# The first pair's masks for both heads by one comparison of 128 partitions, its transfers in another order, its shift rows in two banks, and the last output block bank by bank

## The chip, the cores and the metric

The kernel runs on one core of a Trainium2 chip. The metric is the time of one execution on the device in microseconds (us), as the median of several runs. The profile is of one further execution; its span, from the first to the last instruction, is a little shorter than that execution's time.

The engines are PE (matrix multiply; PEld is its weight load), DVE (vector), ACT (scalar, activations), POOL (general) and SP (issues transfers). SP and ACT both issue DMA transfers here, each in the order of its own queue; SPq and ACTq are these issues in the profile.

## The reference

Attention in hash buckets, and then a feed-forward layer with a rational function:

```python
q_bits = (np.einsum('bhsd,dk->bhsk', q, proj) > 0)      # 6 bits a token; the same for k
mask = q_bucket[:, :, :, None] == k_bucket[:, :, None, :]
scores = np.where(mask, scale * np.matmul(q, k.transpose(0, 1, 3, 2)), -1000000000.0)
attn = np.exp(scores - np.max(scores, axis=-1, keepdims=True))
attn = attn / (np.sum(attn, axis=-1, keepdims=True) + 1e-09)
x = np.matmul(attn, v)                                  # 4 x 8 heads, 768 tokens, 64 each
# x as (3072, 512), then:
h = x @ w_in                                            # 512 -> 2048
g = (a[0] + a[1]*h + a[2]*h**2 + a[3]*h**3) / (1.0 + np.abs(b[0])*np.abs(h) + np.abs(b[1])*h**2 + 1e-6)
out = g @ w_out                                         # 2048 -> 512
```

## The kernel before

Everything is float32; a matmul that must be exact is made from a rounded high part and a low part (qh, ql, kh, kl, gh, gl). The 32 heads are worked in 16 pairs: the two heads of a pair lie on partitions 0 to 63 and 64 to 127. For each pair, `maxstep` makes 12 tiles of scores (psm) on PE, whose row maxima DVE takes (TENSOR_REDUCE, m<-psm); these give each query's shift. `scores` makes them again (pss) in transposed form, ACT takes the exponential (E<-pss), and `values` multiplies with v (psv). The bucket mask is a further matmul of 13 mask rows (mask_q, mask_k) that is added to the same sums, and one more row of mask_q carries the shift, against a row of ones in mask_k.

The mask rows come from the bits: PE multiplies Q and K with the projection (psb; for the first pair psb_first), and DVE compares with zero and subtracts a constant per partition (`TENSOR_SCALAR`, tile mb). For later pairs they are then moved to their partitions by four small transfers on SP (`maskrows`). The first pair uses no such transfers: `first_bits`, `first_compare`, `first_penalties` and `first_k_rows` make its rows in place, in two halves of 384 tokens (HQ), with engines copying head 0's rows to head 1's partitions; `first_shift` turns the maxima into the shift row on PE (pst) and copies it to rows 32 and 96 of mask_q. Until the first data is there, and in gaps, PE runs `warm(n)`: n matmuls on zeros (psw).

The order of all instructions is set by hand: the tables ZERO, ONE and so on hold a place for each step of each pair, `at` files steps by these numbers, and a loop issues them sorted; every engine then keeps program order. PSUM tiles of `ps_b` (tag s) share four banks.

After the last pair comes the feed-forward layer in 6 blocks of 512 tokens. `gemm2` adds the products of 16 parts f into four banks (pso, one for 128 tokens), each part by three matmuls a bank: gh with two weights, gl with one. POOL makes gl from gh. The last block's banks are copied out with a change of sign and stored (`store`).

The transfers at the start, word for word:

```python
queue.dma_start(QF[p][:, halves[0]], qT[p][:, halves[0]])
for c in halves:
    for h in range(2):
        q = nc.scalar if p == 0 and c.start == 0 and h == 1 else queue
        q.dma_start(KF[p][r, c], kT[p][64 - 64 * h : 128 - 64 * h, c])
```

Of the kernel before, what the change touches and what calls it, by code (L numbers as in the profile page):

```python
# [7 lines left out]
F32 = mybir.dt.float32  # L8
F32R = mybir.dt.float32r
# [3 lines left out]
AF = mybir.ActivationFunctionType  # L13
# [37 lines left out]
    penalties=[-94.565, -142.018], compare=-148.248, second=[[-145.217, -148.248], [-149.622, -154.85, -149.024, -148.687]],  # L51
# [99 lines left out]
def bucket_attention_then_rational_ffn(ctx, tc, qT, kT, v, proj, w_in, w_out, coef, consts, out):  # L151
# [70 lines left out]
    last = attention(tc, nc, raw, ps_b, tail, tokens, early, operands_to_terms, ffn, load, QF, KF, v, w_in, w_out, wo_d, ident, cst,  # L222
# [5 lines left out]
def attention(ctx, tc, nc, raw, ps_b, tail, tokens, early, operands_to_terms, ffn, load, QF, KF, v, w_in, w_out, wo_d, ident, cst, ones, prj,  # L228
# [31 lines left out]
    hs = sm.tile([32, 2], F32, name="hs")  # L260
    nc.vector.memset(hs[:, 0:1], 0.0)
    nc.vector.memset(hs[:, 1:2], BIG)
    nc.vector.memset(hs[0:14, 0:1], BIG)
    nc.vector.memset(hs[0:14, 1:2], 0.0)
# [95 lines left out]
    def first_bits(t, hf):  # L360
        if 0 not in MB:
            mb = sm.tile([P, 2, HQ], F32R, tag="mb", name="mb0")
            MB[0], MB[1] = (mb, 0), (mb, 64)
# [12 lines left out]
    def first_penalties(h, hf):  # L376
        rows, bits = MQ[0][64 * h : 64 * h + 32, hf * HQ : hf * HQ + HQ], MB[0][0][0:32, hf, :].bitcast(F32)
        if h == 1 and hf == 0:
            nc.gpsimd.tensor_scalar(out=rows, in0=bits, scalar1=hs[:, h : h + 1], scalar2=None, op0=ALU.mult)
        else:  # L380
            nc.scalar.activation(rows, bits, AF.Identity, scale=hs[:, h : h + 1])

    def first_k_rows(hf):
        c = slice(hf * HQ, hf * HQ + HQ)
        nc.scalar.copy(MK[0][64:96, c], MK[0][0:32, c].bitcast(F32))

    def first_shift(hf):
        c = slice(hf * HQ, hf * HQ + HQ)
        ps = ps_b.tile([P, 512], F32, tag="s", bufs=4, name=f"pst0_{hf}")
        for h in range(2):  # L390
            r = 64 * h + 32
            for i in range(NT // 2):
                j = NT * hf + 3 * h + i
                nc.tensor.matmul(ps[r : r + 1, i * P : i * P + P], M[0][:, j : j + 1], ident, start=True, stop=True)
        for h in range(2):
            r = 64 * h + 32
            if h:
                nc.scalar.activation(MQ[0][r : r + 1, c], ps[r : r + 1, 0:HQ], AF.Copy, scale=-1.0)
            else:
                nc.vector.tensor_scalar(out=MQ[0][r : r + 1, c], in0=ps[r : r + 1, 0:HQ], scalar1=-1.0, scalar2=None, op0=ALU.mult)  # L400
# [12 lines left out]
    def second_compare(hf):  # L413
        nc.vector.tensor_scalar(out=MB[1][0][64:128, hf, :], in0=AV.pop((1, hf))[64:128, 0:HQ], scalar1=0.0,
                                scalar2=cst[64:128, 0:1], op0=ALU.is_gt, op1=ALU.subtract)
# [124 lines left out]
    def at(p, s, f, *args):  # L540
        plan.setdefault(12 * p + s, []).append((f, args))
# [44 lines left out]
    warm(12)  # L586
    for h in range(2):
        nc.gpsimd.memset(MK[0][64 * h + 32 : 64 * h + 33].bitcast(F32), 1.0)
# [4 lines left out]
    for h in range(2):  # L593
        first_penalties(h, 0)
    first_k_rows(0)
# [5 lines left out]
    at(0, ZERO["second"][1][3], first_k_rows, 1)  # L601
# [5 lines left out]
    for hf in range(2):  # L607
        at(0, ZERO["combine"][hf], combine, 0, hf)
        at(0, ZERO["shift"][hf], first_shift, hf)
        at(0, ZERO["penalties"][hf], first_penalties, hf, 1)  # L610
# [4 lines left out]
    at(0, ZERO["compare"], first_compare, 0, 1)  # L615
    at(0, ZERO["clear"], first_clear)
# [77 lines left out]
class Ffn:  # L694
# [49 lines left out]
    def gemm2(self, t, f):  # L744
# [5 lines left out]
        if t == NBLK - 1 and f >= NFC - 2:  # L750
            order.sort(key=lambda ik: ik[1] == 2)
        for i, k in order:
# [5 lines left out]
            if f == NFC - 1 and k == 2:  # L758
                if end and i == n - 1:
                    self.store(t, i, 0, DM // 2, "scalar", nc.scalar)  # L760
                    self.store(t, i, DM // 2, DM, "vector", nc.sync)
                else:
                    self.store(t, i, 0, DM, "vector" if end and i % 2 else "scalar", nc.sync)

    def store(self, t, i, c0, c1, engine, queue):
        nc = self.nc
        if c1 - c0 < DM:
            o = self.tp.tile([P, DM], F32, tag="h2", name=f"oh{c0}_{t}_{i}", bufs=2)[:, 0 : c1 - c0]
        else:
            tag, bufs = ("sr", 1) if i % 3 == 2 else ("xo", 2)  # L770
            o = self.rows.tile([P, DM], F32, tag=tag, name=f"o{t}_{i}", bufs=bufs)[:, 0 : c1 - c0]
        ps = self.sums[t, i][:, c0:c1]
# [5 lines left out]
        queue.dma_start(self.out[r0 : r0 + P, c0:c1], o)  # L778
# [85 lines left out]
```

## Time and profile before

| | |
|---|---|
| median of 3 runs | 920.34 us (920.22 to 920.88) |
| the profiled execution | 919.83 us, its span 917.7 us |
| PE busy | 909.5 us, 99% of the span |
| DVE, ACT, POOL busy | 828.9, 654.4, 364.6 us (90%, 71%, 40%) |
| instructions | 15836 |

The page gives busy time by engine; PE is at work nearly all the time. Every instruction has the line of one helper (L140), so groups are told apart by tile names. In the timeline a row gives start, duration, engine, operation, output<-inputs with their shapes, and a count when several are merged; in brackets stand the idle time of the engine ahead of it and what ended it.

### The profile page before, as it was taken

The numbers are of one execution on the slowest core, as the hardware profiler recorded it, in microseconds if no ns is written. First come the engines' busy times: TensorE is split into PE (matmuls) and PEld (weight loads), VectorE is DVE, ScalarE is ACT, GpSimd is POOL, SyncE is SP. The second block draws the span as 40 slices with busy tenths as digits, with TensorE's granted clock in tenths as the row PEclk, the third lists the DMA queues.
The fourth block names the chain that finished last, engine by engine and source line by source line (L and its number), as shares of the span: only waits on it lengthen the run. The fifth ranks groups of instructions, "written<-read, shape, count | busy, mean of one in ns | idle before, by whom it ended". The sixth has DMA issues, their size and how long they took to land.

```text
span 917.7 us, 15836 instructions
## 1 busy us (share of the span) xinstructions
PE 909.5 (99%) x5838; PEld 725.5 (79%) x5838; DVE 828.9 (90%) x1062; ACT 654.4 (71%) x1228; POOL 364.6 (40%) x349
## 2 busy tenths in 40 slices
PE   9999999999999999999999999999999999999997
PEld 5678777787777787678888888888888888888886
DVE  7788889888988889898999999999999989998996
ACT  5577777777777777786777766776677676777664
POOL 6765655555555555412222232222222222222222
PEclk9999999999999999999999999999999999999999
DMA  6334444444444435355204000400040012001001
GB/s 170 89 125 146 147 144 148 145 149 142 151 141 152 142 118 173 120 197 194 103 1 132 7 0 1 139 1 1 7 131 1 1 62 77 1 1 46 1 0 46
DMA packets 39548, 81.50 MB, mean 89 GB/s; under 512 B 7216, under 2 KB 18596, under 8 KB 39472
## 3 DMA queue, kind: packets, MB, share of 16 engines
q1 hardware_dynamic: 38960, 80.18, 27.1%
q8 instruction: 46, 0.75, 0.3%
q10 hardware_dynamic: 512, 0.33, 0.1%
q14 instruction: 30, 0.25, 0.1%
HBM read 56.82 MB, written 21.17 MB: 85 GB/s over the span
## 4 chain that ended last, share of the span: by engine, by line
PE 95%; DMA 2%; DVE 2%; SPq 1%; ACT 1%; issue 0%; ACTq 0%
PE psh L140 29%; PE pso L140 28%; PE pss L140 13%; PE psv L140 13%; PE psm L140 7%; PE psu L140 2%; PE psb L140 1%; SPq L140 1%; DMA wo_d<-wr 1%; DMA mask_k<-mb 1%; PE psw L140 1%; DMA wr<-w_in 0%; ACT E L140 0%; DVE m L140 0%; DVE ws L140 0%
## 5 line engine op out<-in xcount | busy, mean ns | idle before, releaser
L140 POOL TENSOR_TENSOR gl<-c,gh 128x512 fp32r<-128x512 f32 x96 | 135.8, 1415 | 386.7 <-ACT gh L140 381.2
L140 PE MATMUL pso<-wo,gh 128*128 128x512 f32 x768 | 235.4, 389 | 0.0
L140 DVE TENSOR_REDUCE m<-psm 128x2 f32<-128x768 f32 x192 | 182.5, 958 | 19.6 <-PE psm L140 5.7
L140 ACT ACTIVATE E<-pss 128x384 f32<-128x384 f32 x384 | 167.1, 495 | 34.4 <-PE pss L140 27.7
L140 POOL TENSOR_TENSOR acc<-E,E 128x384 f32<-128x384 f32 x124 | 124.1, 1022 | 148.4 <-ACT E L140 147.6
L140 PEld LDWEIGHTS pso<-wo,gh 128*128 128x128 f32 x768 | 144.1, 188 | 29.8
L140 ACT ACTIVATE h<-psh 128x512 f32<-128x512 f32 x96 | 57.4, 598 | 130.9 <-PE psh L140 130.8
L140 PE MATMUL psh<-xh,wi_hi 128*128 128x512 f32 x384 | 149.6, 390 | 0.0
L140 PE MATMUL psh<-xl,wi_hi 128*128 128x512 f32 x384 | 149.4, 389 | 0.0
L140 PE MATMUL psh<-xh,wi_lo 128*128 128x512 f32 x384 | 149.4, 389 | 0.0
L140 PE MATMUL pso<-wo,gl 128*128 128x512 f32 x384 | 148.4, 389 | 0.0
L140 DVE SCALAR_TENSOR_TENSOR c<-c,ab,r 128x512 f32<-128x512 f32 x96 | 136.6, 1423 | 0.0
L140 PE MATMUL psv<-E,v 128*64 128x385 f32 x768 | 131.3, 490 | 0.0
L140 PEld LDWEIGHTS psv<-E,v 128*64 128x64 f32 x768 | 73.3, 137 | 45.9 <-issue 32.2
L140 POOL TENSOR_TENSOR acc<-acc,E 128x384 f32<-128x384 f32 x96 | 90.0, 958 | 4.0 <-ACT E L140 3.7
L140 DVE SCALAR_TENSOR_TENSOR w<-h,absb,w 128x512 f32<-128x512 f32 x96 | 75.0, 781 | 14.1 <-ACT w L140 13.7
L140 PEld LDWEIGHTS psh<-xh,wi_hi 128*128 128x128 f32 x384 | 72.1, 188 | 16.2 <-DVE c L140 0.6
L140 PEld LDWEIGHTS pso<-wo,gl 128*128 128x128 f32 x384 | 72.2, 188 | 15.0
L140 PEld LDWEIGHTS psh<-xl,wi_hi 128*128 128x128 f32 x384 | 72.1, 188 | 14.8
L140 PEld LDWEIGHTS psh<-xh,wi_lo 128*128 128x128 f32 x384 | 72.0, 188 | 15.0
L140 DVE SCALAR_TENSOR_TENSOR w<-w,r 128x512 f32<-128x512 f32 x96 | 78.5, 818 | 0.0
L140 ACT ACTIVATE c<-psh,ab 128x512 f32<-128x512 f32 x96 | 75.0, 781 | 0.7 <-POOL gl L140 0.7
(93 smaller groups left out, 1539.8 us busy)
## 6 DMA issues: line engine op xcount, KB each, us to landing
wr<-w_out SPq DMA_DIRECT2D x16, 512.0 KB
wr<-w_in SPq DMA_DIRECT2D x16, 512.0 KB
wo_d<-wr SPq DMA_DIRECT2D x16, 512.0 KB
wo<-wo_d SPq DMA_DIRECT2D x16, 512.0 KB
v<-v SPq DMA_DIRECT2D x16, 384.0 KB
x_d<-xo SPq DMA_DIRECT2D x32, 192.0 KB
out<-o SPq DMA_DIRECT2D x23, 256.0 KB
qkf<-qT SPq DMA_DIRECT2D x15, 384.0 KB
```

What stands on the lines that cost most here:

```text
L140: return self.tc.keep_in_program_order(issue(*args, **kwargs))
```

## The change

Four things change, all in the first 25 us or in the last 8.

1. *Masks of the first pair.* `first_bits` makes the bits of both heads: one bank for each of Q, K and each half, a matmul on zeros over all 128 partitions, and then one matmul with the projection for each head, into partitions 0 to 31 and 64 to 95. One comparison of 128 partitions with a new constant tile `first` gives all rows of both heads, the row of ones among them; one ACT instruction with `hs` gives the penalties of both heads. The copies of K's rows on ACT, the head-1 penalty on POOL, the memsets of the ones rows and the memset of the first mask tiles go. The second pair's mb is a tile of its own (mb1), which takes the place of the first's when that has been read. Of the 12 warm-ups ahead of the first bits 6 stay, and each of the two bits brings one matmul on zeros.
2. *Transfers.* Q's first half is issued by ACT, all of K by SP, prj after them; `first` comes by two small transfers on ACT, and cst by SP ahead of the second pair's Q and K.
3. *Shift rows.* `first_shift` writes the two heads' rows into two banks, and DVE copies head 0's, ACT head 1's.
4. *The last step.* In the last f of the last block, gl's matmuls of banks 0 and 1 follow directly on their gh ones, and banks 2 and 3 are then finished one by one. The last bank is copied whole by ACT and stored from ACT's queue, instead of in halves by ACT and DVE.

```diff
-        queue.dma_start(QF[p][:, halves[0]], qT[p][:, halves[0]])
+        (nc.scalar if p == 0 else queue).dma_start(QF[p][:, halves[0]], qT[p][:, halves[0]])
         for c in halves:
             for h in range(2):
                 r = slice(64 * h, 64 * h + 64)
-                q = nc.scalar if p == 0 and c.start == 0 and h == 1 else queue
-                q.dma_start(KF[p][r, c], kT[p][64 - 64 * h : 128 - 64 * h, c])
+                queue.dma_start(KF[p][r, c], kT[p][64 - 64 * h : 128 - 64 * h, c])
...
+    load(0)
     prj = cpool.tile([P, 2, 32], F32, name="prj")
     nc.scalar.dma_start(prj, proj)
-    load(0)
+    first = cpool.tile([P, 2], F32, name="first")
+    for h in range(2):
+        r = 64 * h + 32
+        nc.scalar.dma_start(first[r - 32 : r], consts[r - 32 : r + 32, 0:1].rearrange("(t r) o -> r (t o)", t=2))
+        nc.vector.memset(first[r : r + 32], 0.0)
+        nc.vector.memset(first[r : r + 1, 1:2], -1.0)
     cst = cpool.tile([P, 2 + P], F32, name="cst")
-    nc.scalar.dma_start(cst, consts)
+    nc.sync.dma_start(cst, consts)
...
-    for i in range(3):
+    for i in range(1, 3):
         for m in MASKS:
-            (nc.vector if i == 0 else nc.gpsimd).memset(m[i].bitcast(F32), 0.0)
+            nc.gpsimd.memset(m[i].bitcast(F32), 0.0)
...
     def first_bits(t, hf):
-        if (0, t) not in MS:
-            MS[0, t] = ps_b.tile([P, 512], F32, tag="s", bufs=4, name=f"psb_first{t}")
-        o = 64 * hf + 32 * t
-        nc.tensor.matmul(MS[0, t][o : o + 32, 0:HQ], prj[:, 0, :], (QF, KF)[t][0][:, hf * HQ : hf * HQ + HQ], start=True, stop=True)
+        ps = MS[0, t, hf] = ps_b.tile([P, 512], F32, tag="s", bufs=4, name=f"psb_first{t}_{hf}")
+        nc.tensor.matmul(ps[:, 0:HQ], spare[:, 0:P], spare[:, P:512], start=True, stop=True)
+        for h in range(2):
+            nc.tensor.matmul(ps[64 * h : 64 * h + 32, 0:HQ], prj[:, 0, :], (QF, KF)[t][0][:, hf * HQ : hf * HQ + HQ],
+                             start=True, stop=True)
 
     def first_compare(t, hf):
-        o = 64 * hf + 32 * t
...
-        out = MK[0][0:32, c] if t else MB[0][0][0:32, hf, :]
-        nc.vector.tensor_scalar(out=out, in0=MS[0, t][o : o + 32, 0:HQ], scalar1=0.0, scalar2=cst[o : o + 32, 0:1],
+        out = MK[0][:, c] if t else MB[0][:, hf, :]
+        nc.vector.tensor_scalar(out=out, in0=MS.pop((0, t, hf))[:, 0:HQ], scalar1=0.0, scalar2=first[:, t : t + 1],
                                 op0=ALU.is_gt, op1=ALU.subtract)
 
-    def first_penalties(h, hf):
...
+    def first_penalties(hf):
+        nc.scalar.activation(MQ[0][:, hf * HQ : hf * HQ + HQ], MB[0][:, hf, :].bitcast(F32), AF.Identity, scale=hs)
...
     def first_shift(hf):
-        ps = ps_b.tile([P, 512], F32, tag="s", bufs=4, name=f"pst0_{hf}")
+        ps = [ps_b.tile([P, 512], F32, tag="s", bufs=4, name=f"pst0_{hf}_{h}") for h in range(2)]
...
+        nc.vector.tensor_scalar(out=MQ[0][32:33, c], in0=ps[0][32:33, 0:HQ], scalar1=-1.0, scalar2=None, op0=ALU.mult)
+        nc.scalar.activation(MQ[0][96:97, c], ps[1][96:97, 0:HQ], AF.Copy, scale=-1.0)
...
-    warm(12)
-    for h in range(2):
-        nc.gpsimd.memset(MK[0][64 * h + 32 : 64 * h + 33].bitcast(F32), 1.0)
+    warm(6)
...
-            order.sort(key=lambda ik: ik[1] == 2)
+            order.sort(key=lambda ik: (ik[0] > 1 and f == NFC - 1) * (ik[0] + 1) + (ik[1] == 2))
...
-                if end and i == n - 1:
-                    self.store(t, i, 0, DM // 2, "scalar", nc.scalar)
-                    self.store(t, i, DM // 2, DM, "vector", nc.sync)
-                else:
-                    self.store(t, i, 0, DM, "vector" if end and i % 2 else "scalar", nc.sync)
+                last = end and i == n - 1
+                self.store(t, i, "vector" if end and i == 1 else "scalar", nc.scalar if last else nc.sync, last)
```

The table ZERO changes only where steps are gone or joined (penalties has one place, -142.018, and K's copy none).

Three places show what this does to the order on the engines. In the rows, a name ends with the number of its tile; DMAHW0 to DMAHW7 are eight counters that transfers use in turn, so a wait for one is a wait for the landing of an earlier transfer. First ACT's queue at the start, before:

```order
L140 ACT_TABLE_LOAD
L140 DMA prj_70<-proj 128x64
L140 DMA qkf0_72<-kT 64x384
L140 DMA cst_79<-consts 128x130
L140 CAST qh_0_213<-qkf0_72 128x384 [waits DMAHW0_49]
L140 CAST kh_0_219<-qkf0_72 128x384 [waits DMAHW5_49,DMAHW1_49]
L140 ACTIVATE mask_q0_164<-mb0_215,hs_189 32x384 [waits DVE_49]
```

and after:

```order
L140 ACT_TABLE_LOAD
L140 DMA qkf0_70<-qT 128x384
L140 DMA prj_77<-proj 128x64
L140 DMA first_79<-consts 32x2x1
L140 DMA first_79<-consts 32x2x1 [waits DMAHW0_49]
L140 CAST qh_0_210<-qkf0_70 128x384 [waits DMAHW3_49]
L140 CAST kh_0_218<-qkf0_70 128x384 [waits DMAHW1_49]
L140 ACTIVATE mask_q0_171<-mb0_216,hs_194 128x384 [waits DVE_49]
```

K's first half uses counters 0 and 1: the second transfer of `first` waits for the landing of one of its two pieces, and the casts stand behind it.

Second, ACT's queue around the first shift row (pst0), the scaling of the second pair's mb behind it, and the first exponentials (E), before:

```order
L140 ACTIVATE ws1_257<-wr1_256 128x512 [waits DMAHW3_49]
L140 ACTIVATE mask_q0_164<-mb0_215,hs_189 32x384
L140 ACTIVATE mask_q0_164<-pst0_0_319 1x384 [waits DVE_49]
L140 ACTIVATE mb0_215<-mb0_215,cst_79 64x768 [waits DMAHW7_49]
L140 ACTIVATE E3_155<-pss0_3_0_351 128x384 [waits PE_49]
```

and after:

```order
L140 ACTIVATE mask_q0_171<-mb0_216,hs_194 128x384 [waits DVE_49]
L140 ACTIVATE ws1_257<-wr1_256 128x512 [waits DMAHW5_49]
L140 ACTIVATE mask_q0_171<-pst0_0_1_324 1x384 [waits PE_49,Activation_49]
L140 ACTIVATE mb1_293<-mb1_293,cst_86 64x768 [waits DMAHW1_49,DVE_49,Activation_49]
L140 ACTIVATE E3_162<-pss0_3_0_356 128x384 [waits PE_49]
```

The shift row's wait for DVE has become one for PE, and the wait for DVE stands at mb.

Third, PE's last part (wo15; pso5_0 to pso5_3 are the four banks), before:

```order
L140 MATMUL pso5_0_9665<-wo15_5800,gh5_15_10187 128x512 [waits Activation_49]
L140 MATMUL pso5_0_9665<-wo15_5800,gh5_15_10187 128x512
L140 MATMUL pso5_1_9669<-wo15_5800,gh5_15_10187 128x512 x2
L140 MATMUL pso5_2_9673<-wo15_5800,gh5_15_10187 128x512 x2
L140 MATMUL pso5_3_9677<-wo15_5800,gh5_15_10187 128x512 x2
L140 MATMUL pso5_0_9665<-wo15_5800,gl5_15_10188 128x512 [waits Pool_49]
L140 MATMUL pso5_1_9669<-wo15_5800,gl5_15_10188 128x512
L140 MATMUL pso5_2_9673<-wo15_5800,gl5_15_10188 128x512
L140 MATMUL pso5_3_9677<-wo15_5800,gl5_15_10188 128x512
```

and after:

```order
L140 MATMUL pso5_0_9671<-wo15_5806,gh5_15_10193 128x512 [waits Activation_49]
L140 MATMUL pso5_0_9671<-wo15_5806,gh5_15_10193 128x512
L140 MATMUL pso5_1_9675<-wo15_5806,gh5_15_10193 128x512 x2
L140 MATMUL pso5_0_9671<-wo15_5806,gl5_15_10194 128x512 [waits Pool_49]
L140 MATMUL pso5_1_9675<-wo15_5806,gl5_15_10194 128x512
L140 MATMUL pso5_2_9679<-wo15_5806,gh5_15_10193 128x512 x2
L140 MATMUL pso5_2_9679<-wo15_5806,gl5_15_10194 128x512
L140 MATMUL pso5_3_9683<-wo15_5806,gh5_15_10193 128x512 x2
L140 MATMUL pso5_3_9683<-wo15_5806,gl5_15_10194 128x512
```

The wait for POOL's gl moves from the ninth matmul of this part to the fifth, and the banks end after 5, 6, 9 and 12 matmuls instead of 9 to 12.

More of the change, by code (lines that the diff above doesn't have):

```diff
@@ L50 @@
     scores=[-76.211, -72.938, -71.772, -78.557, -67.007, -32.505, -32.485, -6.609, 3.148, 0.944, 1.776, 8.766],
-    penalties=[-94.565, -142.018], compare=-148.248, second=[[-145.217, -148.248], [-149.622, -154.85, -149.024, -148.687]],
+    penalties=-142.018, compare=-148.248, second=[[-145.217, -148.248], [-149.622, -154.85, -149.024]],
     low=[[-95, -75.382], [-149.619, -93.811]], clear=23.614, warms=[1, 1, 1, 1, 1, 1],
@@ L221, in bucket_attention_then_rational_ffn @@
     tail.tile([P, 32], F32, tag="below", name="below")
-    last = attention(tc, nc, raw, ps_b, tail, tokens, early, operands_to_terms, ffn, load, QF, KF, v, w_in, w_out, wo_d, ident, cst,
+    last = attention(tc, nc, raw, ps_b, tail, tokens, early, operands_to_terms, ffn, load, QF, KF, v, w_in, w_out, wo_d, ident, cst, first,
                      ones, prj, wi_hi, wi_lo, x_d, s_d, r_d, coefficients)
@@ L227, in attention @@
 @with_exitstack
-def attention(ctx, tc, nc, raw, ps_b, tail, tokens, early, operands_to_terms, ffn, load, QF, KF, v, w_in, w_out, wo_d, ident, cst, ones, prj,
+def attention(ctx, tc, nc, raw, ps_b, tail, tokens, early, operands_to_terms, ffn, load, QF, KF, v, w_in, w_out, wo_d, ident, cst, first, ones, prj,
               wi_hi, wi_lo, x_d, s_d, r_d, coefficients):
@@ L258, in attention @@
     WARM = []
[L260 to L264, printed above, removed]
+    hs = sm.tile([P, 1], F32, name="hs")
+    nc.vector.memset(hs, 0.0)
+    nc.vector.memset(hs[0:14], BIG)
+    nc.vector.memset(hs[64:96], BIG)
+    nc.vector.memset(hs[64:78], 0.0)
     QH, KH, QL, KL, V, MB, ACC, EXP, AV, MS = ({} for _ in range(10))
@@ L369, in first_compare @@
+        nc.tensor.matmul(ps[:, 0:HQ], spare[:, 0:P], spare[:, P:512], start=True, stop=True)
+        for h in range(2):
+            nc.tensor.matmul(ps[64 * h : 64 * h + 32, 0:HQ], prj[:, 0, :], (QF, KF)[t][0][:, hf * HQ : hf * HQ + HQ],
+                             start=True, stop=True)
     def first_compare(t, hf):
-        o = 64 * hf + 32 * t
         c = slice(hf * HQ, hf * HQ + HQ)
-        out = MK[0][0:32, c] if t else MB[0][0][0:32, hf, :]
-        nc.vector.tensor_scalar(out=out, in0=MS[0, t][o : o + 32, 0:HQ], scalar1=0.0, scalar2=cst[o : o + 32, 0:1],
+        if t == 0 and 0 not in MB:
+            MB[0] = sm.tile([P, 2, HQ], F32R, tag="mb", name="mb0")
@@ L393, in first_shift @@
                 j = NT * hf + 3 * h + i
-                nc.tensor.matmul(ps[r : r + 1, i * P : i * P + P], M[0][:, j : j + 1], ident, start=True, stop=True)
-        for h in range(2):
[L396 to L400, printed above, removed]
+                nc.tensor.matmul(ps[h][r : r + 1, i * P : i * P + P], M[0][:, j : j + 1], ident, start=True, stop=True)
+        nc.vector.tensor_scalar(out=MQ[0][32:33, c], in0=ps[0][32:33, 0:HQ], scalar1=-1.0, scalar2=None, op0=ALU.mult)
+        nc.scalar.activation(MQ[0][96:97, c], ps[1][96:97, 0:HQ], AF.Copy, scale=-1.0)
     def first_clear():
@@ L413, in second_compare @@
     def second_compare(hf):
+        if 1 not in MB:
+            MB[1] = sm.tile([P, 2, HQ], F32R, tag="mb", name="mb1"), 64
         nc.vector.tensor_scalar(out=MB[1][0][64:128, hf, :], in0=AV.pop((1, hf))[64:128, 0:HQ], scalar1=0.0,
@@ L584, in attention @@
         at(NPAIR - 1, x, ffn.step, f)
-    warm(12)
-    for h in range(2):
-        nc.gpsimd.memset(MK[0][64 * h + 32 : 64 * h + 33].bitcast(F32), 1.0)
+    warm(6)
     for t in range(2):
@@ L592, in attention @@
         first_compare(t, 0)
-    for h in range(2):
-        first_penalties(h, 0)
-    first_k_rows(0)
+    first_penalties(0)
     warm(4)
@@ L600, in attention @@
     at(0, ZERO["second"][1][2], first_compare, 1, 1)
-    at(0, ZERO["second"][1][3], first_k_rows, 1)
     for t in range(2):
@@ L609, in attention @@
         at(0, ZERO["shift"][hf], first_shift, hf)
-        at(0, ZERO["penalties"][hf], first_penalties, hf, 1)
         at(1, ONE["combine"][hf], combine, 1, hf)
@@ L615, in attention @@
     at(0, ZERO["compare"], first_compare, 0, 1)
+    at(0, ZERO["penalties"], first_penalties, 1)
     at(0, ZERO["clear"], first_clear)
@@ L758, in gemm2, with store @@
             if f == NFC - 1 and k == 2:
-                if end and i == n - 1:
-                    self.store(t, i, 0, DM // 2, "scalar", nc.scalar)
-                    self.store(t, i, DM // 2, DM, "vector", nc.sync)
-                else:
-                    self.store(t, i, 0, DM, "vector" if end and i % 2 else "scalar", nc.sync)
-    def store(self, t, i, c0, c1, engine, queue):
-        nc = self.nc
[L767 to L772, printed above, removed]
+                last = end and i == n - 1
+                self.store(t, i, "vector" if end and i == 1 else "scalar", nc.scalar if last else nc.sync, last)
+    def store(self, t, i, engine, queue, last):
+        nc = self.nc
+        tag, bufs = ("sr", 1) if i % 3 == 2 else ("xo", 2)
+        o = self.tile("h2", t, NFC) if last else self.rows.tile([P, DM], F32, tag=tag, name=f"o{t}_{i}", bufs=bufs)
+        ps = self.sums[t, i]
         if engine == "scalar":
@@ L777, in store @@
         r0 = t * NTK + i * P
-        queue.dma_start(self.out[r0 : r0 + P, c0:c1], o)
+        queue.dma_start(self.out[r0 : r0 + P], o)
     def step(self, i):
```

10 lines of the change are left out of this document (removed).

## The prediction

> **What bounds the kernel now.** I read the page first, then the busy time by stage, the waits of PE, and the chain of waits and the timeline at both ends, where the change lies.
>
> ```profile
> span 917.7 us, 15836 instructions
> ```
> ```profile
> 8.50:17.20 8.70, 7.99 (x58) 3.65 (x56) 8.40 (x13) 4.39 (x7) 6.71 (x6) 1.00 0.47 144
> ...
> 40.00:880.00 840.00, 839.72 (x5414) 675.40 (x5413) 770.74 (x981) 611.34 (x1151) 328.21 (x299) 1.00 0.28 89
> ```
>
> The columns of the second fence are the stretch, its length, and busy time of PE, PEld, DVE, ACT and POOL. From 40 to 880 us PE idles 0.28 us of 840: whatever PE gains before 40 us reaches the end nearly whole, and nothing else counts there. From 8.5 to 17.2 us DVE is the bound (8.40 of 8.70). Between the two stands one long wait, in the waits of PE (total, times, longest):
>
> ```profile
> PE psm L140 <- DMA mask_k<-mb: 1.2, 2, 0.9
> ```
>
> The chain of waits shows what that transfer hangs on (start, us, what):
>
> ```profile
> 16.53 0.62 DVE mb L140
> ...
> 17.77 0.48 ACT mask_q L140
> ...
> 18.27 0.93 ACT mb L140
> ...
> 21.86 2.33 DMA mask_k<-mb
> ```
>
> The second pair's masks (mb) go to its rows by four small transfers on SP, the last landing at 24.19. ACT can scale mb from 17.15 on, when DVE has made it, but it does so at 18.27: ahead of it in ACT's queue stands the first pair's shift row of head 1, and that waits for DVE's copy of head 0 (the row at 17.77 below), since both lie in one bank.
>
> **The change part by part.** Rows of the timeline at the start (start, us, engine, what; the idle time before it and its releaser in brackets):
>
> ```profile
> 1.25 3.68 PE L140 MATMUL psw<-E 128*128 128x384 bf16 x12 [1.25 <-DVE E L140]
> 1.78 0.85 ACTq L140 DMA_DIRECT2D cst<-consts  x1
> 3.36 0.51 ACT L140 CAST qh<-qkf 128x384 fp32r<-128x384 f32 x1 [1.34 <-DMA qkf<-qT]
> 5.21 0.51 ACT L140 CAST kh<-qkf 128x384 fp32r<-128x384 f32 x1 [1.34 <-DMA qkf<-kT]
> 5.73 0.60 DVE L140 TENSOR_SCALAR mb<-psb_first,cst 32x384 fp32r<-32x384 f32 x1 [2.59 <-PE psb_first L140]
> 6.00 0.82 PE L140 MATMUL psw<-E 128*128 128x384 bf16 x4
> 7.03 0.83 PE L140 MATMUL psb_first<-qkf,prj 128*32 128x384 f32 x2 [0.21 <-DVE mask_k L140]
> 7.90 0.62 DVE L140 TENSOR_SCALAR mask_k<-psb_first,cst 32x384 fp32r<-32x384 f32 x1 [0.93 <-PE psb_first L140]
> 8.55 1.83 DVE L140 TENSOR_REDUCE m<-psm 128x2 f32<-128x768 f32 x2
> 10.73 0.83 ACT L140 CAST kh<-qkf 128x768 fp32r<-128x768 f32 x1 [0.32 <-DMA qkf<-kT]
> 11.53 1.48 PE L140 MATMUL psb<-qkf,prj 128*32 128x384 f32 x8
> 12.91 0.62 DVE L140 TENSOR_SCALAR mb<-psb,cst 64x384 fp32r<-64x384 f32 x1
> 15.68 1.04 PE L140 MATMUL pst<-cst,m 128*1 128x128 f32 x12 [0.35 <-DVE m L140]
> 16.76 0.60 SPq L140 DMA_DIRECT2D v<-v  x1
> 17.77 0.48 ACT L140 ACTIVATE mask_q<-pst 1x384 fp32r<-1x384 f32 x1 [4.18 <-DVE mask_q L140]
> 19.23 0.94 SPq L140 DMA_DIRECT2D mask_q<-mb  x1
> ```
>
> *Shift rows in two banks: -1.0 us.* PE's twelve pst matmuls end at 15.68 + 1.04 = 16.72. ACT's row then needs no DVE: 16.76 to 17.24 by its 0.48. The scaling of mb starts at 17.27 (DVE's 17.15 is earlier) instead of 18.27, and SP's first mask transfer, which starts at 19.23 right behind it, at 18.23; SP's load of v ahead of it was issued by 17.36. With the same four issues the last lands at 23.19. Would PE be there? Here are its last two matmuls ahead of the masks:
>
> ```profile
> 23.08 0.34 PE L140 MATMUL psm<-mask_k,mask_q 64*128 64x384 f32 x1
> 24.32 0.41 PE L140 MATMUL psm<-mask_k,mask_q 64*128 64x384 f32 x1 [0.91 <-DMA mask_k<-mb]
> ```
>
> PE stood ready at 23.41, and earlier once ACT's row and exponentials no longer hold it up around 18 to 20 us. So it still waits for the DMA, a little less, and gains what the DMA gains: 1.0.
>
> *The start of the DVE stretch: 0.0 to -0.1 us.* DVE's queue from 8.55 on holds the same number of instructions as before. A comparison took 0.60 to 0.62 us on 32 partitions and 0.62 on 64, so I price it on 128 at 0.62. The whole stretch therefore moves with its first TENSOR_REDUCE at 8.55. Two lines of work end there:
> - DVE's own: three comparisons back to back, 3 x 0.65 = 1.95 us from the first, without the 0.93 idle, since the K halves lie in banks of their own. The first one starts when the first bits and the new constants (first) are there.
> - PE's: psb_first of Q, of K, four warm-ups, psb_first of K's second half, psm. A psb_first for both heads is two matmuls into different 32-column groups; the eight records of psb (four matmuls, two such pairs) took 1.48, so 0.76 a pair, hardly more than one alone (7.03 to psm at 7.79). Each brings one zeroing matmul, priced by the warm-ups (0.16 from start to start, and 0.1 for the change of form): 0.26. From the start of the Q bits: 0.76 + 0.26 + 0.76 + 0.66 (warm-ups) + 0.26 + 0.76 = 3.46 to psm; before it was 2.93 (4.86 to 7.79).
>
> When do Q's bits start? Seven of the first matmuls remain: 7 x 0.32 = 2.3 us, to about 3.75 (E's memset moves some 0.2 us behind the four new small ones on DVE). Q landed by 3.36 when it was alone in front; now K's first piece shares its time on SP, and prj comes behind it on ACT. Bounds: 3.4 (nothing lost) and 5.2 (as late as K on the second place). I take 4.05, nearer to the row of the same transfer. Some of it runs at the slow clock (below), 0.2. Then psm starts at 4.05 + 0.2 + 3.46 = 7.71 against 7.79, and DVE's third comparison and reduce 0.08 earlier. Bounds for this term: -0.5 and +0.9.
>
> The removed work frees engines but not the path: POOL's head-1 penalty, ACT's copy of K's mask, POOL's ones rows and two large DVE memsets free their engines ahead of that reduce; none of them stands in the two lines above, so they are priced at nothing.
>
> *Queues moved.* SP now carries cst ahead of the second pair's Q and K, and each of those waits for an earlier transfer. They are issued about 1 us later. ACT's cast of that K waited for its landing at 10.73; behind it ACT makes the penalties of the second half, which must now end before DVE's comparison at 12.91, since the second pair's mb takes the tile of the first. Cast 0.83 and penalty 0.61: K must land by 11.4. Between nothing and the full 1 us of the later issue reaches the landing: 10.7 to 11.7, which costs between nothing and 0.3. I take nothing, since the transfers are queued well ahead of their landing.
>
> *The last step bank by bank: -1.0 us.* The end (second fence: bytes moved, from 912.7 us in 40 slices of 0.125 us):
>
> ```profile
> 909.48 1.29 POOL L140 TENSOR_TENSOR gl<-c,gh 128x512 fp32r<-128x512 f32 x1 [1.39 <-issue]
> 909.97 1.98 PE L140 MATMUL pso<-wo,gh 128*128 128x512 f32 x8
> ...
> 911.78 1.07 PE L140 MATMUL pso<-wo,gl 128*128 128x512 f32 x4
> 912.21 1.08 ACT L140 ACTIVATE o<-pso 128x512 f32<-128x512 f32 x2 [2.86 <-PE pso L140]
> ...
> 912.83 1.31 SPq L140 DMA_DIRECT2D out<-o  x3
> ...
> 914.23 0.40 SPq L140 DMA_DIRECT2D out<-oh  x1
> ```
> ```profile
> GB/s 0 0 0 0 0 0 0 115 328 442 377 410 410 394 410 377 442 377 328 393 393 410 459 344 475 360 336 369 344 99 0 0 0 0 0 0 0 0 0 0
> ```
>
> Today all four banks finish within 0.7 us, so 1.05 MB leaves in one burst at about 400 GB/s, from 0.75 us after the first issue to 916.4; the span ends 1.25 us later. In the new order the first gl matmul is the fifth, at 909.97 + 4 x 0.227 = 910.88, but gl is ready at 910.77 and its weights load 0.2 ahead: +0.15 for all that follow. The first bank's transfer is then issued at about 912.1 instead of 912.83, and the last matmul starts at 912.62. ACT takes its bank 0.43 later, 0.60 long, and issues at 913.67. From there: 0.75 to 1.2 us to the first byte, 256 KB at 400 GB/s 0.65, and 1.25 to the end: 916.3 to 916.8. The earlier three are out of the way by then. I take 916.7, a gain of 1.0; the bounds are 0.3 (if the last transfer needs as long as the 3.47 us from 914.23 to 917.7, and 0.33 for its larger size) and 1.3.
>
> **Sum.** 917.7 - 1.0 - 0.05 - 1.0 = 915.65 of span. The profiled execution took 919.83, 2.13 more than its span; the median of the runs shown, 920.34, is 0.5 above it. From the median: 920.34 - 2.05 = 918.3.
>
> **The rivals.**
> 1. *The clock.* The first matmuls start 0.32 us apart (12 in 3.68), the four at 6.00 0.16: PE runs at half speed until about 4.4 us. With 7 instead of 12 in front and a gap before Q's bits, the full clock may come one such period of some 3.2 us later. PE's line to psm then takes about 1.3 us more, and all that follows moves: 918.3 + 1.3 = 919.6. For it: the new gap. Against it: PE is still busy most of that period. [...]
> 2. *The constants come late (the other side).* ACT issues two transfers for first, and the second waits for one of K's first pieces; ACT's casts stand behind it. K's landing of 5.21 and the 2.33 of a small transfer give 7.5, and DVE's reduce 1.95 later: 9.5, +0.9, time 919.3. It decides against the change if the transfer takes as long as cst's did at most (1.78 to 5.73, 3.95): 9.2, reduce at 11.1, +2.6, time 920.9. Below 6.4 it costs nothing, which I expect, since K now goes first on SP and may land near 3.4.
> 3. *The tail stays a burst.* If the last transfer takes as long as today's, the tail gives 0.3: 919.0.
> 4. *The DMA chain does not move*, because SP or the rings are still busy with v: 919.3. Against it: SP had nothing to issue from 17.36 to 19.23.
>
> **How the numbers follow.** Forecast 0.60, clock 0.14, late constants 0.12 (of which 0.04 slower than before by over 0.2%), tail 0.08, chain 0.06. Times differing by 0.2% (1.84 us) are about the least that a measurement of this kernel can tell from no change, so the limit is 918.5, just beyond the forecast: of its 0.60, the terms' bounds leave 0.50 below 918.5 and 0.10 above; with the rivals that makes 0.50 faster, 0.46 within, 0.04 slower. The range reaches from 917.4 (both ends of the first 10 us and the tail at their better bounds) to 919.6, the clock rival.
>
> **What would show it.** Right: ACT's shift row ahead of DVE's, mb scaled near 17.3, PE's wait for mask_k ending near 23.2, four issues of out spread over 1.6 us, 915.6 of span. Wrong: a first reduce on DVE later than 8.7, DVE waiting for ACT near 12.9, warm-ups 0.32 apart after 5 us, or the first comparison released by a DMA after 6.4.

## The result and the profile after

The changed kernel took 930.95 us (median of 4 runs, 929.57 to 934.25) against 920.61 (920.22 to 921.07) for the kernel before, run on the same chip: a ratio of 1.0117, 95% interval 1.0090 to 1.0144. Forecast were 918.3 us in a range of 917.4 to 919.6, and a chance of 0.04 for slower. The profiled execution took 930.87, its span is 10.8 us longer. Head of the page, and the two stretches that the prediction showed (length; busy time and count of PE, PEld, DVE, ACT, POOL; granted clock):

```profile
span 928.5 us, 15841 instructions
```
```profile
8.50:17.20 8.70, 7.98 (x57) 3.67 (x57) 7.82 (x11) 3.29 (x5) 5.32 (x4) 1.00 0.62 194
40.00:880.00 840.00, 837.15 (x5367) 664.41 (x5367) 765.68 (x969) 603.94 (x1140) 323.27 (x297) 1.00 0.28 89
```

PE is nearly as busy as it was (837.15 us of 840 against 839.72) and its clock is 1.00, but in the same 840 us it did 5367 matmuls instead of 5414. So the loss lies where the prediction said that nothing counts. The waits of PE name two small places:

```profile
PE psm L140 <- DMA mask_k<-mb: 2.3, 2, 1.2
PE pso L140 <- ACT o L140: 1.5, 1, 1.5
```

The rest is no wait at all. Here is the chain of waits in the middle of the FFN, of the kernel before (its blocks are alike) and then of the changed one, in an odd block of tokens (523 us) and in an even one (601 us). Each row is one product of twelve matmuls, psh the first and pso the second:

```profile
602.77 2.72 PE psh L140 x12
605.49 2.72 PE pso L140 x12
```
```profile
523.43 2.73 PE psh L140 x12
526.16 2.79 PE pso L140 x12
...
601.11 2.77 PE psh L140 x12
603.88 2.80 PE pso L140 x12
```

Twelve matmuls took 2.72 us before (227 ns each) and take up to 2.80 now (233 ns). A step of 24 goes from 5.44 to 5.57 us in even blocks and 5.52 in odd ones. Ninety-six steps make (48 x 0.13) + (48 x 0.08) = 10 us by these rounded rows; laid side by side, matmul by matmul, the 2304 matmuls of the FFN drift apart by 10.1 us in this way.

So the 10.8 us of span come from: -0.2 up to the start of the FFN (a loss at the start and at 46 us, a gain at the shift rows and along the attention); +10.1 from the slower matmuls; +1.8 from one stall at 757 us; -0.9 from the last matmul to the end, the gain of the tail.

The start (timeline: start, us, engine, what; idle time before and its releaser in brackets):

```profile
1.66 2.10 PE L140 MATMUL psw<-E 128*128 128x384 bf16 x6 [1.66 <-DVE hs L140]
4.24 1.49 PE L140 MATMUL psb_first<-qkf,prj 128*32 128x384 f32 x4 [0.16 <-DMA prj<-proj]
6.51 0.62 DVE L140 TENSOR_SCALAR mb<-psb_first,first 128x384 fp32r<-128x384 f32 x1 [4.30 <-DMA first<-consts]
8.76 0.62 DVE L140 TENSOR_SCALAR mask_k<-psb_first,first 128x384 fp32r<-128x384 f32 x1 [1.07 <-PE psb_first L140]
9.30 1.82 DVE L140 TENSOR_REDUCE m<-psm 128x2 f32<-128x768 f32 x2
14.61 1.82 DVE L140 TENSOR_REDUCE m<-psm 128x2 f32<-128x768 f32 x2 [0.48 <-PE psm L140]
16.69 1.04 PE L140 MATMUL pst<-cst,m 128*1 128x128 f32 x12 [0.36 <-DVE m L140]
17.83 0.48 ACT L140 ACTIVATE mask_q<-pst 1x384 fp32r<-1x384 f32 x1 [3.86 <-PE pst L140]
18.34 0.93 ACT L140 ACTIVATE mb<-mb,cst 64x768 fp32r<-64x768 f32 x1
```

ACT's shift row now waits for PE's pst alone, as intended. But DVE's first reduce starts at 9.30 instead of 8.55 (the comparison ahead of it waits 1.07 for PE's bits, the first four of which run at the slow pace, 1.49), and DVE waits 0.48 for PE at 14.61, so that this reduce comes 5.31 behind the first where it was 5.05 (8.55 to 13.60). The last mask transfer ends at 24.49, 0.30 later than before, and the third pair's, further on in the chain, took 3.26 us where it took 2.33; below it the stall at 757:

```profile
22.16 2.33 DMA mask_k<-mb
...
44.91 3.26 DMA mask_k<-mb
```
```profile
757.70 4.25 DMA out<-o
```

The end, and the bytes from 923.5 us on in 40 slices of 0.125 us:

```profile
922.92 0.60 ACT L140 ACTIVATE o<-pso 128x512 f32<-128x512 f32 x1 [2.29 <-PE pso L140]
...
923.54 1.31 SPq L140 DMA_DIRECT2D out<-o  x3
...
924.12 0.39 PE L140 MATMUL pso<-wo,gl 128*128 128x512 f32 x1
924.54 0.60 ACT L140 ACTIVATE h<-pso 128x512 f32<-128x512 f32 x1
925.17 0.37 ACTq L140 DMA_DIRECT2D out<-h  x1
```
```profile
GB/s 0 0 0 0 0 0 0 360 344 426 344 442 328 393 344 442 344 377 394 344 442 344 442 328 410 360 410 344 361 66 0 0 0 0 0 0 0 0 0 0
```

From the last matmul's start to the end of the span are 4.4 us instead of 5.2. The bytes still leave in one burst, which only starts earlier against the last matmul.

### The profile page after: what moved, and what is told of

Read it like the earlier page. It is cut to its first block, busy times and chain, and to the rows that moved or that the text cites. A ratio compares the mean times of both kernels' runs of the same rounds, so it can differ in the third digit from the quotient of the medians.

```text
span 928.5 us, 15841 instructions
## 1 busy us (share of the span) xinstructions
PE 918.0 (99%) x5844; PEld 722.7 (78%) x5844; DVE 831.8 (90%) x1063; ACT 652.8 (70%) x1225; POOL 359.8 (39%) x346
## 4 chain that ended last, share of the span: by engine, by line
PE 94%; DMA 2%; DVE 1%; SPq 1%; ACT 1%; issue 0%; ACTq 0%
PE pso L140 28%; PE psh L140 28%; PE pss L140 13%; PE psv L140 13%; PE psm L140 7%; PE psu L140 2%; PE psb L140 1%; SPq L140 1%; DMA wo_d<-wr 1%; DMA mask_k<-mb 1%; PE psb_first L140 1%; DMA out<-o 0%; DMA wr<-w_in 0%; DVE m L140 0%; DMA prj<-proj 0%
## 5 line engine op out<-in xcount | busy, mean ns | idle before, releaser
L140 POOL TENSOR_TENSOR gl<-c,gh 128x512 fp32r<-128x512 f32 x96 | 133.5, 1391 | 400.5 <-ACT gh L140 399.1
L140 PE MATMUL pso<-wo,gh 128*128 128x512 f32 x768 | 240.7, 395 | 1.5 <-ACT o L140 1.5
L140 PE MATMUL pso<-wo,gl 128*128 128x512 f32 x384 | 150.8, 394 | 0.0
L140 DVE SCALAR_TENSOR_TENSOR c<-c,ab,r 128x512 f32<-128x512 f32 x96 | 139.8, 1456 | 0.0
L140 DVE SCALAR_TENSOR_TENSOR w<-h,absb,w 128x512 f32<-128x512 f32 x96 | 72.9, 760 | 21.9 <-ACT w L140 21.7
```

What stands on the lines that cost most here:

```text
L140: return self.tc.keep_in_program_order(issue(*args, **kwargs))
```

## Experiments: the slower matmuls

What does an edit of the first and last 10 us do to the FFN's matmuls? The edits add one tile, first, of 8 bytes in a pool ahead of the weights, where a tile takes 32. By the addresses in the built programs, everything that is allocated behind it on the left side of SBUF lies 32 bytes higher: wi_hi 17536 to 17568, wo 108160 to 108192, x of the odd blocks 173696 to 173728. The tiles of the right side (gh and gl, x's last quarter in even blocks) stay. In the kernel before, the distance from every streamed operand of the FFN to the weights that PE loads for it is a multiple of 512 bytes. Also, the two buffers of x have swapped places. Theory A: the addresses. Theory B: something that the edits do.

**e1_after_64**, the changed kernel (the two transfers and memsets take `[..., 0:2]` of the tile):
```
-    first = cpool.tile([P, 2], F32, name="first")
+    first = cpool.tile([P, 16], F32, name="first")
...
```


> The changed kernel with nothing altered but the size of the new tile first: 16 columns instead of 2, of which 2 are used, so that all tiles behind it lie 64 bytes higher than in the kernel before, instead of 32. Theory A (addresses): the new tile pushed the FFN's operands from multiples of 64 bytes to 32 beyond one, and PE's matmuls there go 226-227 to about 233 ns apart; with 64 bytes they are back at 226-227 ns, the 2.2 us stall at 757 us goes with them or not, and the time is 918.5 to 921.5. Theory B (the edits: the two x buffers in swapped places, another order of transfers, ACT's and DVE's phase against PE): all of that is still there, the spacing stays near 233 ns and the time at 930 to 931.

926.14 us, 1.0060 (1.0043 to 1.0077): neither forecast (the profiled execution took 928.99; its rows are read for the pace alone). In odd blocks psh is back at 2.72 and pso at 2.75; even blocks stay slow:

```profile
521.50 2.75 PE pso L140 x12
524.25 2.72 PE psh L140 x12
...
604.27 2.79 PE pso L140 x12
607.07 2.77 PE psh L140 x12
```

So not the multiple of 64 of each address, but the addresses do matter: in odd blocks both operands of psh moved by 64 together.

**e2_before_32**, the kernel before, with a tile behind qbias that is never used:
```
+    pad = cpool.tile([P, 8], F32, name="pad")
```


> The kernel before with one unused tile of 32 bytes ahead of the weights: every instruction is the same, and the addresses behind it are those of the changed kernel (but for the two x buffers, which stay in their old places). Theory A: the FFN's matmuls go about 233 ns apart and the time rises by 9 to 11.5 us, to 929 to 932. Theory B: 226-227 ns, 920.3 within 0.5.

929.98 us, 1.0103 (1.0088 to 1.0118). Not one instruction differs from the kernel before but in addresses, and nearly the whole loss is there, with the same rows as in the changed kernel:

```profile
601.45 2.77 PE psh L140 x12
604.22 2.80 PE pso L140 x12
```

The swap of x's buffers, which is not in this run, plays no part, and theory B falls for this share.

**e3_wo_32**, the kernel before (first fence), and **e4_wi_32**, the kernel before (second):
```
+        ctx.enter_context(tc.tile_pool(name="gap0", bufs=1)).tile([P, 8], F32, name="gap0")
         wp = ctx.enter_context(tc.tile_pool(name="wp", bufs=1))
+        ctx.enter_context(tc.tile_pool(name="gap1", bufs=1)).tile([P, 8], F32, name="gap1")
```
```
+    cpool.tile([P, 8], F32, name="pad")
...
     wi_lo = wpool.tile([P, NCC, DFF], F32R, name="wi_lo")
+    wpool.tile([P, 8], F32, name="pad2")
```


> The kernel before with 32 bytes ahead of the wo tiles (the moving operand of the FFN's second product) and 32 more behind them, so that wo alone lies 32 beyond a multiple of 64, and x of the odd blocks is back on one. Theory A, if it is the moving operand's address that counts: only pso slows, by 6 to 7 ns in each of 1152 matmuls: +7 to +8 us, 927.3 to 928.4. Theory A', if it needs both operands of a matmul, or the weights' address: no change, 920.3. Theory B: 920.3.

> The kernel before with 32 bytes ahead of wi_hi and wi_lo (the weights that PE loads for the FFN's first product) and 32 more behind them, so that they alone lie 32 beyond a multiple of 64 and all else on one. If it is the address of the moving operand that counts, no change: 920.3 within 0.7. If it is that of the loaded weights, psh slows as it did in the changed kernel's blocks 0, 2 and 4 (231 to 234 ns): 576 matmuls by 4 to 7 ns, +2.3 to +4 us, or twice that if it strikes all blocks: 922.6 to 928.4. Theory B: 920.3.

e3 931.11 us, 1.0114 (1.0099 to 1.0129); e4 933.55, 1.0143 (1.0128 to 1.0158): the worst of all, and both slower than any forecast made for them. Chain of e3, then of e4:

```profile
602.25 2.76 PE psh L140 x12
605.01 2.80 PE pso L140 x12
```
```profile
601.97 2.80 PE psh L140 x12
604.77 2.75 PE pso L140 x12
```

Only PE reads wo and wi in the FFN. Moving wo away from gh and gl slows pso (2.80 instead of 2.72); moving wi away from x slows psh (2.80). And in e3's even blocks psh is slow (2.76) though its own operands lie as before: its first seven matmuls start 224 to 241 ns apart, its last five 227, so in this trace it took seven matmuls behind a slow product to fall back into step. In e3's odd blocks x has moved by both gaps, 64 bytes, and wi has not: psh is slow there throughout (2.75). That is why e3 costs more than pso alone. In e4 the two tiles move wo by 64 bytes as well, and pso is slow too. Hence theory A'': what counts is the distance between a streamed operand and weights that PE loads meanwhile.

**e5_after_fit**, the changed kernel:
```
-    absb1 = cpool.tile([P, 1], F32, name="absb1")
-    qbias = cpool.tile([P, 1], F32, name="qbias")
+    both = cpool.tile([P, 2], F32, name="both")
+    absb1, qbias = both[:, 0:1], both[:, 1:2]
```


> The changed kernel with two one-column tiles (absb1 and qbias) put into one, which frees the 32 bytes that first takes: the weights and all tiles behind them are back at the addresses of the kernel before; the two x buffers stay in swapped places, and every step of the change is in. Theory A'' (the distance between a matmul's streamed operand and the weights that PE loads, which was a multiple of 512 bytes for all pairs in the FFN of the kernel before, sets its pace): 226-227 ns everywhere, no stall at 757 us, and what the three steps bring by themselves: 917.8 to 919.6. If something else in the change slows the FFN too (the swap, the order of transfers), it stays above 922.

**e6_after_right_32**, the changed kernel, in which nothing returns to its old place:
```
-PAD = 352
+PAD = 320
```


> The changed kernel with 32 bytes less of the pad at the other end of SBUF, so that the tiles kept there (gh and gl, which PE loads as weights in the second product, and the last quarter of x of the even blocks) move up by 32 as well. All operands are then 32 beyond a multiple of 64, but the distances between them are those of the kernel before. Theory A'' (distances): 226-227 ns everywhere, 917.8 to 920. Theory A (each address by itself): unchanged, 930 to 931.

e5 922.57 us, 1.0020 (1.0011 to 1.0029); e6 922.08, 1.0016 (1.0007 to 1.0026). In both the products take 2.72 us again, psh and pso (in e6 all but those at the stall of the next section); of e6:

```profile
604.53 2.72 PE pso L140 x12
```

e6 decides between address and distance: every operand is 32 beyond a multiple of 64, all distances are as before, and the pace is full. Moving one pad by 32 bytes brought 9 us back. Both are still slower than before by some 1.5 to 2 us, and miss their forecasts, so a second cause remained.

How far do distances count? **e7_before_right_256** and **e15_before_right_128**, the kernel before with PAD = 96 and PAD = 224:

> The kernel before with that pad smaller by 256 bytes: gh, gl and the last quarter of x of the even blocks lie 256 bytes higher, all else in its place. If distances count modulo 256 or less (but for 64, which slowed pso to 228-230 ns in the first experiment's odd blocks): no change, 920.3. If they count modulo 512: pso and a quarter of psh slow down, by 2 to 7 ns each, 923 to 929.

> The kernel before with the right side's pad smaller by 128 bytes: gh, gl and the last quarter of x of the even blocks 128 bytes higher. If distances count modulo 128: no change, 920.4. If modulo 256: pso at 229 to 234 ns, 923 to 929.

e7 920.16 us, 0.9996 (0.9986 to 1.0006), all products 2.72. e15 929.57 (2 runs), 1.0098 (1.0078 to 1.0118):

```profile
603.78 2.78 PE pso L140 x12
```

So in these runs 256 bytes are free (2.72 in e7), and 32 (2.80 in e3's pso), 64 (2.75 in e1's, odd blocks) and 128 (2.78 in e15's) cost: by distance alone, a matmul took 227 ns or up to 233. Whether it is the weights of this matmul or the next that disturb it, and in what part of SBUF, was not tried. A hint is in the odd blocks of the changed kernel and of e2: the last matmul of psh, with its own weights in place and the next ones, gh, 32 bytes off, takes 235 ns (median), the eleven ahead of it 226 to 227; the last of pso, where it is the other way round, takes 226 to 227. But in even blocks that one takes 233, so the hint does not settle it.

## Experiments: the stall and the late masks

The stall in the timeline of ACT, before and after: the fourth o of a block takes the buffer of the first, so it waits until the first has been stored.

```profile
753.32 0.60 ACT L140 ACTIVATE o<-pso 128x512 f32<-128x512 f32 x1 [1.26 <-DMA out<-o]
```
```profile
762.04 0.60 ACT L140 ACTIVATE o<-pso 128x512 f32<-128x512 f32 x1 [3.40 <-DMA out<-o]
```

What delays that transfer? The DMA view of the stretch in which its first bytes move (751.7 to 752.8 before, 758.3 to 759.4 after; queue, packets, MB, share):

```profile
q1 hardware_dynamic: 179, 0.33, 78.8%
```
```profile
q1 hardware_dynamic: 167, 0.31, 74.3%
q8 instruction: 1, 0.02, 9.7%
```

A packet of instruction code (16 KB) sits on one of the 16 DMA engines (9.7% of 16 engines for 1.1 us, 1.7 us of one); as we read it, what the transfer has on that engine comes behind it. Before, it came after the first transfer. Over the whole run this queue carries 46 such packets, 0.75 MB: if it is PE's code, about 64 bytes for each of the 5844 matmuls and 5844 weight loads, an estimate. Theory C: this packet makes the stall. Theory D: its place goes by the number of instructions that PE has issued. The change gives PE six more matmuls at the start (four zeroing ones and eight more for the bits, against six warm-ups less; with a weight load each, 12 instructions). Another such packet then falls into the third pair's masks at 46 us (the DMA view from 44.9 to 48.2 us has one).

**e10_fit_own_o**, e5 with:
```
-        tag, bufs = ("sr", 1) if i % 3 == 2 else ("xo", 2)
+        tag, bufs = (("xo", 2), ("xo", 2), ("sr", 1), ("o3", 1))[i]
```


> The changed kernel at the old addresses (as in e5_after_fit), and the fourth o of each block in a buffer of its own, so that ACT needn't wait there until the first o's transfer has landed. Theory C (a packet of instruction code, 16 KB on one of the 16 DMA engines, falls into that transfer at 754 to 758 us and delays its landing; ACT waits 3 to 3.5 us for the buffer and PE behind it): the stall of 1.6 us is gone, 922.6 becomes 920.7 to 921.2. If something else held PE there: no change, 922.2 to 922.8.

921.05 us, 1.0002 (0.9993 to 1.0011); ACT's wait is gone (the stall it ended had cost 1.6 us in e5's trace), and the chain runs through:

```profile
757.25 2.72 PE psh L140 x12
```

**e11_fit_own_o_fewer_warms**, e10 without the four warm-ups and without two of the six single ones:
```
-    warm(4)
...
+        if i not in (1, 3):
...
```


> The same with six warm-up matmuls less (the four after the first bits, two of the six in DVE's stretch), so that PE has issued as many instructions as in the kernel before when it comes to the second and third pair. Theory D (the code packet that falls into the third pair's mask transfers at about 46 us, and costs about 1 us there, came 12 PE instructions earlier in the program than in the kernel before): the packet is back behind that transfer, which takes 2.33 instead of 3.3 to 3.7 us, -1.0; and the first reduce starts up to 0.6 earlier: 919.2 to 920.2. If the position of that packet doesn't hang on the number of PE's instructions: the transfer stays at 3.3 or more, 920.1 to 921.2. If fewer warm-ups keep PE at half pace: the start is later by 0.5 to 1.5, 921 to 922.

918.76 us, 0.9981 (0.9972 to 0.9990). The third pair's masks take 2.32 us, and in that time the DMA view has no packet of q8:

```profile
43.12 2.32 DMA mask_k<-mb
```

The first reduce also starts early in this trace, at 8.00; the four warm-ups had stood in PE's line to it. To tell the count from the start, **e13_before_12_more**, the kernel before:
```
-        for _ in range(n):
-            nc.tensor.matmul(ps[:, 0:HQ], spare[:, 0:P], spare[:, P:512], start=True, stop=True)
+        for k in range(n + 6 * (n == 12)):
+            c = HQ if k < n else 2
+            nc.tensor.matmul(ps[:, 0:c], spare[:, 0:P], spare[:, P : P + c], start=True, stop=True)
```


> The kernel before with six tiny matmuls (2 columns each) behind the first twelve warm-ups: 12 more PE instructions (6 weight loads, 6 matmuls), as the changed kernel has, and some 0.3 to 1.0 us more in front; nothing else. Theory D: the code packet of 49.4 us moves to 46 to 47 and into the third pair's mask transfers, which take 3.2 to 3.7 us instead of 2.33 (+1), and the one of 753.6 to about 752, into the first o's transfer: ACT waits there 3 us or more instead of 1.3 (up to +2): 921.8 to 924. If the place hangs on other engines' instructions: packets and transfers as before, 920.8 to 921.6.

923.32 us, 1.0036 (1.0023 to 1.0049), with both delays in the kernel before (chain, DMA view from 45.3 to 48.6 us, waits):

```profile
45.32 3.20 DMA mask_k<-mb
```
```profile
q8 instruction: 1, 0.02, 2.0%
```
```profile
ACT o L140 <- DMA out<-o: 7.9, 5, 3.2
```

Six matmuls that compute nothing cost 2.8 us. In the trace it is 0.7 at the start (first reduce 9.25, within the scatter shown below), 0.9 at the third pair and 1.8 at the stall. A late start alone does not do this: in e2, e7 and e8, whose PE issues as many instructions as before, the first reduce comes 0.6 to 1.0 later, yet the third pair's masks take 2.32 to 2.40 us and ACT's longest wait for an o is 1.3. PE's wait at the stall stands in the five traces with the added instructions and the shared buffer (the changed kernel, e1, e5, e6, e13) and in no other. For PE no wait for code shows in these traces, but a transfer beside such a packet is late (3.20 us in e13 instead of 2.33).

In e6 the stall cost more than its wait: PE idled 1.78 us there, and from 756 us on the granted clock was 0.50 for 3.4 us, eight matmuls 0.43 us apart, which cost another 1.6 us; behind the shorter idle times of the four others, 1.3 to 1.5 us, the clock stayed at 1.00. Of e6 (columns as in the stretches above):

```profile
756.00:758.00 2.00, 2.00 (x6) 1.54 (x5) 1.69 (x3) 1.97 (x4) 0.00 (x0) 0.50 0.97 295
```

## Experiments: the steps of the change by themselves

**e8_tail_alone** and **e9_banks_alone**, the kernel before with only the diff's part of the last step, and only that of first_shift:

> The kernel before with the last step bank by bank alone (the order of the last twelve matmuls and the storing of the four banks); addresses unchanged. By the prediction's term -1.0 us (bounds -0.3 and -1.3): 919.2 to 919.9 if before is at 920.2. By the changed kernel's trace, where 4.4 us pass from the last matmul's start to the end of the span against 5.2 before, and the order costs 0.15: -0.7. If the tail stays a burst: -0.3 or less.

> The kernel before with the shift rows in two banks alone; addresses and PE's instruction count unchanged. The prediction's term: ACT's shift row at the end of the twelve pst matmuls, the mask transfers 1.0 us earlier, PE's wait for them with it, -1.0 us: 919.3 to 919.7 with before at 920.4. What the changed kernel's trace and those of two experiments show between the first pair's and the second pair's start (0.45 to 0.7 us regained): -0.5 to -0.7. If PE then waits a little later for the third pair's masks: no change.

e8 919.71 us, 0.9992 (0.9983 to 1.0000), by the medians 0.8 less. From the last matmul (913.59) to the end of the span (918.0) 4.41 us pass, 0.83 less than before, and the order costs 0.06. e9 919.90, 0.9992 (0.9984 to 1.0001): its executions scatter from 918.70 to 921.63, so by time alone its gain of 0.7 is not told from nothing. The profile, of the fastest of them, starts as the kernel before's does (first reduce 8.53) and can be compared; its timeline and chain:

```profile
16.72 0.48 ACT L140 ACTIVATE mask_q<-pst 1x384 fp32r<-1x384 f32 x1 [3.16 <-PE pst L140]
...
17.23 0.93 ACT L140 ACTIVATE mb<-mb,cst 64x768 fp32r<-64x768 f32 x1
18.19 0.94 SPq L140 DMA_DIRECT2D mask_q<-mb  x1
```
```profile
20.81 2.33 DMA mask_k<-mb
```

Each is the forecast within 0.05 us (16.76, 17.27, 18.23, landing 23.19: here 23.14), and all that follows, to the end, is 1.05 us earlier.

**e14_before_layout**, the kernel before with the pad of e2 and PAD = 320, and **e12_best**, the changed kernel with the edits of e10 and e11 and PAD = 320:

> The kernel before, its instructions untouched, in the layout of e6_after_right_32 and e12_best: all tiles of the left side and those of the FFN's right side 32 bytes higher, the attention's right side in its place. If the attention's gain is the layout's: from the third to the last pair about 1.2 us less, FFN at 226-227 ns, 919.1 to 919.6. If it is the change's: 920.5. What then lies between this run and e12 is what the change and its two repairs bring: about 2.3.

> The same edits in the layout of e6_after_right_32 (left and right tiles both 32 bytes up), in which the attention took about 1.2 us less from the third to the last pair, with the FFN at 226-227 ns: 918.0 to 919.0, below the kernel before by 1.4 to 2.4 us. If that gain was not the layout's: 919.2 to 920.2.

e14 919.82 us, 0.9992 (0.9982 to 1.0001): with a first reduce 1.0 later than in the kernel before's profile its span is the same 917.7. So the attention gains about a microsecond from 32 bytes by which its left tiles move against its right ones: from 60 us to the FFN the five traces in that layout (the changed kernel, e2, e6, e12, e14) gain 0.8 to 1.3 us on the kernel before, the nine without that shift nothing (0 to 0.3 lost). Which operands do it was not tried. e12 917.01, 0.9962 (0.9950 to 0.9975), the fastest of all. Against e14, in the same layout, the change with its two repairs brings (1 - 0.9962/0.9992) x 920.5 = 2.8 us.

## Why the prediction was wrong

**The step that failed first** is in its opening: whatever PE gains before 40 us reaches the end nearly whole, "and nothing else counts there". The first half held (e9's 1.05 us arrive at the end undiminished). The second half left out that an edit outside that stretch can change the pace in it. No term and no rival stood for the addresses that the new tile moves, or for the number of PE's instructions. Measured: +10.1 us for the pace in the changed kernel's trace (e2, with the instructions unchanged, 9.75 of time), +1.8 for the stall and +0.9 for the third pair's masks (what e10, e11 and e13 take away or bring).

**Shift rows in two banks, -1.0**: right, -1.05 alone. In the changed kernel it is -0.45, since DVE waits 0.48 for PE at 14.61, and the second issue on SP takes 1.04 instead of 0.81. The prediction counted DVE's queue there, but not the zeroing matmul and the second pair of bits that PE has ahead of it.

**Start of DVE's stretch, -0.05**: too good, +0.75 in the changed kernel's profile. The term that was too small is PE's line: from Q's bits (4.24) to the first psm (8.64) it took 4.40 us, where 3.46 and 0.2 for the slow clock were priced. The last comparison ahead of the reduce waited 1.07 us for these bits, and 0.7 to 1.1 in the four other traces with this start and all its warm-ups, so this is rival 1: the trace's record of the granted clock begins, at full, at 6.3 us, and at 4.4 in the profile before. What brings the full clock no run shows. Rival 2 is there but hidden: the constants land late (6.51, with 6.4 named as the point from which they cost), yet DVE then idles for PE. Only with e11's fewer warm-ups (e11, e12) do the comparisons follow on the constants back to back.

How much the start costs, one trace cannot say: the same start takes a different time in each execution. With the edits undone, nine traces show the first reduce at 8.53 to 9.55, mean 9.08; five with the changed start 8.75 to 9.94, mean 9.51: +0.4, less than the scatter. The pace of PE's first matmuls changes at another time in each execution: the trace's record of the granted clock begins, at full, at 4.4 us in e9 and at 7.3 in e8, and the reduce comes at 8.53 and at 9.55. Here is e8, whose start is that of the kernel before, as is e9's, where the first four bits took 1.10 and the reduce came at 8.53:

```profile
1.25 4.02 PE L140 MATMUL psw<-E 128*128 128x384 bf16 x12 [1.25 <-DVE E L140]
5.20 1.64 PE L140 MATMUL psb_first<-qkf,prj 128*32 128x384 f32 x4
9.55 1.82 DVE L140 TENSOR_REDUCE m<-psm 128x2 f32<-128x768 f32 x2
```

The prediction's 8.55 was near the early end of what the same code does.

**The last step, -1.0**: right in kind; -0.77 in the trace of e8. The last transfer was priced at 0.65 us of bytes behind its issue, as if the three others were out of the way; the row of bytes shows one burst to the end, so it gets a share.

**The sum**: with the two side effects taken away, e11 has the three steps and less warm-up: 0.9981, 1.8 us gained where 2.05 were forecast. That it is so close is partly luck: e10, with all warm-ups, gained nothing (1.0002), or some 0.9 if the third pair's delay is taken off, which is an estimate; the rest of e11's gain goes with the warm-ups that it leaves out, which the prediction did not forecast. What was missing above all is what the edits do to things that they don't name. **Rivals**: 3 and 4 did not come about (the tail gave 0.77, and e9's DMA chain moved by all of 1.05).

## What to carry to other kernels

Before costing the steps of a change, list what it shifts without naming it: the addresses of all tiles behind a new or resized one, and the number of instructions per engine. A kernel whose matmuls run back to back can be on a lucky layout (here 227 ns a matmul, and up to 233 off it); add a tile where it moves nothing, or pad so that the distances between streamed operands and weights stay, and look at the pace of twelve matmuls in the chain first. When a wait for a buffer hangs on one transfer's landing, a packet of code can make it longer (here 3.40 us instead of 1.26, nearly three times); a buffer of its own is cheaper than finding out.

## What was not expected of the hardware

- The pace of this kernel's fp32 matmuls of 128x512 in the FFN went with the distance in SBUF between the streamed operand and the weights: 227 ns with the distances of the kernel before (also in e5, e6 and e14) or 256 bytes off them (e7), up to 233 on the average of twelve at 32, 64 or 128 off (e2, e3, e1, e15), with no wait in the profile and the clock at 1.00.
- A 16 KB packet of instruction code took 1.7 us of one DMA engine, and the wait for the 256 KB store that it fell into was 3.40 us instead of 1.26.
- Behind an idle time of PE of 1.78 us in the middle of the run, the granted clock was 0.50 for 3.4 us (e6).
- The first 10 us of the same code scatter by 1.0 us between executions (first reduce at 8.53 in e9, 9.55 in e8), with the time from which the full clock is granted (4.4 and 7.3).
